# Two weight loads of a cached-attention decode kernel sent in narrow transfers

## The chip, the core and the metric

One core of a Trainium2 chip runs the program. The metric is the device time of one execution in microseconds; the median of three runs before the change is 2498.54 us (2498.37 to 2499.15).

## The reference

Two layers, each an attention block over a cache and a token-mixing block, for a batch of two tokens of width 512, with 32 query heads, 8 cache heads, a cache of 32768 positions and head width 128:

```python
q = (layernorm(x) @ wq)                       # per head of 128
scores = q . k_cache * Dh ** -0.5             # 4 query heads share one cache head
x = x + softmax(scores) @ v_cache @ wo
h = layernorm(layernorm(x))                   # then the mixer, over the token axis
x = x + gelu(h * w1 + b1) @ w2 + b2
```

The caches of keys and values are read in both layers, 268 MB each, in float32; the weights are small beside them.

## The kernel before, in words

All that the loads bring goes into one tile `mem` of 106 cells, each 512 floats wide on all 128 partitions. A unit is one layer, batch and cache head. Its keys (kind K, from `kt`) are 64 cells, its values (kind V, from `v`) as many. A head's `wq` and `wo` parts are 4 cells each (2048 floats, 8 KB on a partition, 1 MB in all), from `wqo`. PE multiplies cell by cell as they come: `k_step` (L360) writes scores, `v_step` (L428) sums up the values, `make_q` makes a unit's queries from `wq` (L325 is its wide product, ten steps of four cells ahead of the unit's first key).

The order of all work is a list of steps written by `Order`: the keys of a unit, then the values of the unit before. `plan_loads` goes through it ahead of time and gives each load a size (32 cells at most, which is 8 MB) and a place among the 106 cells; weights are asked for 16 steps ahead (`ASK_Q`). Some cells are kept over at the two places where a layer ends and the next begins (about 1000 to 1460 us); there the loads are of 4 cells and less. All loads are issued on SP's queue in the planner's order by `load` (L877 weights, L882 caches), each when PE has done with what stood in its cells. The loads take eight completion semaphores in turn (DMAHW0 to DMAHW7 below), and a load waits for the last one that used its semaphore, unless another of its waits covers that. Small inputs and one output row go over ACT's queue.

Each of these loads has 128 partitions, and the sixteen DMA engines take eight rows each; a row is one packet. An engine's part ends in a packet of 4 bytes, which counts up the load's semaphore. PE's instructions come over the same engines (queue q8).

Of the kernel before, what the change touches and what calls it, by code (L numbers as in the profile page):

```python
# [13 lines left out]
P = 128  # L14
G = 512
# [23 lines left out]
STEP_US = 1.6  # L39
ASK_Q = 16  # L40
ASK_O = 8


class Order:
# [158 lines left out]


@with_exitstack
def gqa_mixer_kernel(ctx: ExitStack, tc: tile.TileContext, x, kt, v, wqo, cols, out):
    nc = tc.nc
    B, D = out.shape
    HKV = wqo.shape[0]
# [21 lines left out]
    def cells(a, n):  # L231
        return mem[:, a * G : (a + n) * G]
# [538 lines left out]
    for u in order.units:  # L771
        layer, b, h = u
# [11 lines left out]
    for name, us in users.items():  # L784
        k0 = min(first["K", u] for u in us)
        h = name if isinstance(name, int) else name[1]
# [3 lines left out]
        weights.append((k0 - ASK_Q if k0 else -1, ("q", layer, h), max(first["K", u] for u in us) if both else k0))  # L790
        weights.append((k0 if both else v0 + ASK_O, ("o", layer, h), max(end["V", u, 1] for u in us) + 3))

    for u in order.units:
        layer, b, h = u
# [76 lines left out]
    def load(label, n, a):  # L871
        kind, u, g = label
        if kind == "W":
            part, layer, h = u
            w = D * R
            at_w = 0 if part == "q" else w
            nc.sync.dma_start(cells(a, n), wqo[h][:, at_w : at_w + w])  # L877
            (wq_sb if part == "q" else wo_sb)[layer, h] = cells(a, n).rearrange("p (t c) -> p t c", t=DT)
            return
        layer, b, h = u  # L880
        src = (kt if kind == "K" else v)[b * HKV + h, g // HALF, :, (g % HALF) * G : (g % HALF + n) * G]
        nc.sync.dma_start(cells(a, n), src)  # L882
        for j in range(n):
            at_cell[kind, u, g + j] = a + j
            if (kind, u, g + j) in order.kept:
                at_cell[order.kept[kind, u, g + j]] = a + j
# [5 lines left out]
    for label, n, a in begin.get(-1, ()):  # L892
        load(label, n, a)
# [4 lines left out]
    for p, (kind, u, g) in enumerate(steps):  # L898
        (k_step if kind == "K" else v_step)(u, g)
        for f, args in hooks.pop(p, ()):  # L900
            f(*args)
        for label, n, a in begin.get(p, ()):
            load(label, n, a)
# [3 lines left out]
def _layout(A_x, A_k_cache, A_v_cache, A_wq, A_wo, B_w1, B_b1, B_w2, B_b2):  # L907
    import numpy as np

    B, HKV, SK, DH = A_k_cache.shape  # L910
    D = A_x.shape[-1]
    U = B * HKV
    kt = A_k_cache.reshape(U, 2, NG, 32, 2, 2, 8, 2, 2, DH).transpose(0, 1, 9, 4, 7, 8, 2, 5, 6, 3)
    wq = A_wq.reshape(D // P, P, HKV, -1).transpose(2, 1, 0, 3)
    wo = A_wo.reshape(HKV, -1, DH, D).transpose(0, 2, 1, 3)
    w1, b1, w2 = (a.reshape(P, -1) for a in (B_w1, B_b1, B_w2))
    none = np.zeros_like(w2)
    w2z = np.stack([none, w2], axis=2).reshape(P, -1)
    cols = [w1, b1, w2z, none[:, :1], np.broadcast_to(B_b2.reshape(1, 1), (P, 1))]
    return {  # L920
        "x": np.ascontiguousarray(A_x.reshape(B * (D // P), P).T),
        "kt": np.ascontiguousarray(kt).reshape(U, 2, DH, HALF * G),
        "v": A_v_cache.reshape(U, 2, P, HALF * G),
        "wqo": np.concatenate([wq.reshape(HKV, P, -1), wo.reshape(HKV, DH, -1)], axis=2),
        "cols": np.concatenate(cols, axis=1),
    }


_INS = ["x", "kt", "v", "wqo", "cols"]


# [20 lines left out]
```

## Time and profile before

| what | value |
|---|---|
| profiled execution, device time | 2498.51 us |
| its span, first to last instruction | 2496.7 us |
| moved by DMA | 1064.64 MB, mean 426 GB/s |
| loads on SP's queue (q1) | 34568 packets, 1063.27 MB |
| PE busy | 1335.6 us, 53% |
| mean granted clock of TensorE | 0.765 |
| weight loads | 28, 1024 KB each, median 38.0 us from issue to landing |

The page's DMA line gives the busy share of all sixteen engines in 40 slices of 62.4 us. A query by stretches gives the same share, and GB/s, for any part of the span. Of the time of a single DMA engine there is no view, but the trace holds every packet with its start, duration, size and queue.

### The profile page before, as it was taken

To read this page: it belongs to the slowest core of one execution; us is meant where nothing else is said; L and a number is where in the kernel's file an instruction comes from. 1 tells how busy PE (TensorE), PEld (TensorE's weight loads), DVE (VectorE), ACT (ScalarE), POOL (GpSimd) and SP (SyncE) were. 2 spreads that over 40 slices of the span, in tenths; PEclk is the share of its full clock that TensorE was granted. 3 is DMA by queue.
4 is the path that set the end of the run, shared out by engine and by line. 5 is a ranking of instruction groups with operands and counts; after the bars stand their busy time and mean duration, and the time that the engine had idled before them with its cause. 6 is when DMAs were issued, how large, how long until landed. Compare 5 with 4: busy or idle time off the path is not lost.

```text
span 2496.7 us, 21064 instructions
## 1 busy us (share of the span) xinstructions
PE 1335.6 (53%) x9562; PEld 373.7 (15%) x9562; DVE 211.3 (8%) x599; ACT 186.9 (7%) x581; POOL 5.1 (0%) x18
## 2 busy tenths in 40 slices
PE   3455455444445544556776774454454544554557
PEld 1111111111111111111221221111111111111113
DVE  1000000000000000101110110000000000000012
ACT  0100000000000000000210210000000000000021
POOL 0000000000000000000000000000000000000000
PEclk8777777777777777778887986777677777776788
DMA  9999999999999999999999999999999999999996
GB/s 421 434 433 430 434 431 434 430 431 436 433 427 437 428 434 434 424 436 408 419 429 422 420 427 437 433 433 430 433 434 428 434 432 434 433 433 433 429 433 275
DMA packets 34946, 1064.64 MB, mean 426 GB/s; under 512 B 4133, under 2 KB 4137, under 8 KB 5034
## 3 DMA queue, kind: packets, MB, share of 16 engines
q1 hardware_dynamic: 34568, 1063.27, 99.1%
q8 instruction: 75, 1.23, 0.2%
q14 instruction: 13, 0.11, 0.0%
q10 hardware_dynamic: 290, 0.04, 0.0%
HBM read 1063.29 MB, written 0.00 MB: 426 GB/s over the span
## 4 chain that ended last, share of the span: by engine, by line
DMA 63%; PE 24%; another core or an unknown queue 11%; DVE 1%; issue 0%; ACT 0%; SPq 0%; POOLq 0%; POOL 0%; DVEq 0%; ACTq 0%
DMA mem<-in_v_dram 34%; DMA mem<-in_kt_dram 29%; PE acc L428 15%; PE scores L360 6%; PE misc L332 1%; PE bcast L325 0%; PE rows L492 0%; PE misc L384 0%; PE misc L451 0%; PE misc L657 0%; ACT S L410 0%; PE misc L378 0%; DVE row L462 0%; SPq L882 0%
## 5 line engine op out<-in xcount | busy, mean ns | idle before, releaser
L428 PE MATMUL acc<-mem,S 128*16 128x512 f32 x4080 | 595.5, 716 | 595.4 <-DMA mem<-in_v_dram 587.2
L360 PE MATMUL scores<-mem,qz 128*32 128x512 f32 x4096 | 593.7, 720 | 531.7 <-DMA mem<-in_kt_dram 531.6
L410 ACT ACTIVATE S<-S,neg 128x128 f32<-128x128 f32 x256 | 129.5, 509 | 2212.0 <-DVE S L405 1196.1
L360 PEld LDWEIGHTS scores<-mem,qz 128*32 128x32 f32 x4096 | 141.9, 126 | 910.6 <-issue 820.6
L428 PEld LDWEIGHTS acc<-mem,S 128*16 128x16 f32 x4080 | 127.2, 106 | 907.4 <-issue 827.5
L370 DVE TENSOR_REDUCE mx<-scores 128x1 f32<-128x512 f32 x64 | 44.3, 692 | 795.4 <-PE scores L360 787.6
L405 DVE STREAM_TRANSPOSE S<-scores 128x512 f32<-128x512 f32 x64 | 45.5, 710 | 125.4 <-PE acc L428 125.4
L410 ACT ACTIVATION_READ_ACCUMULATOR S<-S,neg 128x1 f32 x256 | 47.7, 187 | 0.0
L492 PE MATMUL rows<-mem,oz 128*2 128x512 f32 x248 | 46.6, 835 | 0.3 <-DVE oz L481 0.3
L380 DVE TENSOR_REDUCE m<-misc 1x4 f32<-1x128 f32 x32 | 8.9, 279 | 383.3 <-PE misc L378 383.3
L453 DVE RECIPROCAL rl<-misc 128x4 f32<-128x4 f32 x32 | 5.8, 182 | 384.6 <-PE misc L451 384.6
L462 DVE SCALAR_TENSOR_TENSOR row<-acc,quad,row 128x128 f32<-128x128 f32 x96 | 33.7, 351 | 3.4
L460 DVE TENSOR_SCALAR row<-acc,quad 128x128 f32<-128x128 f32 x32 | 11.2, 350 | 174.0 <-PE acc L428 174.0
L481 DVE TENSOR_TENSOR oz<-misc,rl 128x4 f32<-128x4 f32 x32 | 5.2, 161 | 221.3 <-PE misc L471 220.9
L471 PEld LDWEIGHTS misc<-head,row 128*128 128x128 f32 x64 | 14.0, 273 | 52.2 <-issue 38.3
L325 PE MATMUL bcast<-mem,xw 128*32 128x512 f32 x144 | 20.6, 635 | 1.7 <-POOL x_rs L298 1.7
L451 PEld LDWEIGHTS misc<-both,one 128*128 128x128 f32 x64 | 13.6, 266 | 49.9 <-issue 47.0
L471 PE MATMUL misc<-head,row 128*128 128x4 f32 x64 | 16.8, 333 | 7.3 <-DVE row L462 7.3
L332 PEld LDWEIGHTS misc<-selg,row 128*128 128x128 f32 x128 | 17.1, 208 | 20.1 <-issue 11.2
L576 ACT ACTIVATE row<-bcast,bias,scale 128x512 f32<-128x512 f32 x21 | 16.3, 777 | 36.7 <-PE rows L560 13.4
L332 PE MATMUL misc<-selg,row 128*128 128x2 f32 (+1 forms) x128 | 18.5, 266 | 0.8 <-DVE row L317 0.8
L451 PE MATMUL misc<-both,one 128*128 128x4 f32 x64 | 16.4, 327 | 2.0 <-DVE both L450 2.0
(126 smaller groups left out, 277.0 us busy)
## 6 DMA issues: line engine op xcount, KB each, us to landing
mem<-in_v_dram SPq DMA_DIRECT2D x13, 4096.0 KB, 25.5
mem<-in_v_dram SPq DMA_DIRECT2D x37, 1024.0 KB, 9.0
mem<-in_kt_dram SPq DMA_DIRECT2D x15, 2048.0 KB, 17.4
mem<-in_kt_dram SPq DMA_DIRECT2D x30, 1024.0 KB, 8.9
mem<-in_wqo_dram SPq DMA_DIRECT2D x28, 1024.0 KB, 38.0
mem<-in_kt_dram SPq DMA_DIRECT2D x6, 4096.0 KB, 28.7
mem<-in_kt_dram SPq DMA_DIRECT2D x2, 6144.0 KB, 24.1
mem<-in_v_dram SPq DMA_DIRECT2D x3, 2048.0 KB, 38.4
```

Source lines behind the costliest of these rows:

```text
L325: nc.tensor.matmul(q_ps[us][32 * d : 32 * d + 32, :], xw[:, d, :], wq[:, d, :], start=True, stop=True)
L332: nc.tensor.matmul(pt[:, r * n : (r + 1) * n], q_row[us][:, r * DH : (r + 1) * DH], side, start=True, stop=True,)
L360: nc.tensor.matmul(sc_ps[u, half][32 * row : 32 * row + 32, :], qz[:, at : at + 32], cells(at_cell["K", u, g], 1), start=(i == 0), stop=(i ...
L370: nc.vector.tensor_reduce(mx[u][:, half : half + 1], sc_ps[u, half], axis=AX.X, op=ALU.max)
L405: nc.vector.transpose(S[half], sc_ps[u, half])
L410: nc.scalar.activation(s[:, :, h], s[:, :, h], AF.Exp, bias=neg[u][:, h : h + 1], scale=SCALE, accum_out=lsum[u][:, half, h : h + 1],)
L428: nc.tensor.matmul(acc[32 * row : 32 * row + R * QT, :], S[half][:, col : col + R * QT], vc, start=(g < NG), stop=(g >= quads - NG),)
L451: nc.tensor.matmul(pl[:, :R], ones, both, start=True, stop=True)
L462: nc.vector.scalar_tensor_tensor(asb[u], acc[:, t * DH : (t + 1) * DH], quad[:, t : t + 1], asb[u], op0=ALU.mult, op1=ALU.add)
L471: nc.tensor.matmul(po_of[u][:, :R], asb[u], head, start=True, stop=(u != order.last))
L492: nc.tensor.matmul(rows[32 * r : 32 * r + B, :], oT[u][:, 2 * r + 1 - b : 2 * r + 3 - b], wo_of(u)[:, r, :], start=False, stop=(u == order ...
L576: nc.scalar.activation(hid[key, f], px[key], AF.Gelu_apprx_tanh, bias=shift[key][:, f : f + 1], scale=slope[key][:, f : f + 1],)
```

## The change

Two of the 28 weight loads are issued otherwise: `wq` of head 5 in layer 0, and `wq` of head 1 in layer 1. Their partitions 96 to 127 come in one transfer as before (32 rows). Partitions 0 to 95 come in four transfers of 24 partitions, from a new input `narrow`, where the rows lie as six groups of four, with a fifth row of padding behind each group, so that the source's outermost dimension has six members. The change's own words for it are transfers of six DMA engines. Bytes, cells, the plan and the order of all other loads stay as they are.

```diff
+NARROW = (("q", 0, 5), ("q", 1, 1))
+GROUPS = 6
+DEPTH = 4
+PIECES = 4
...
-            nc.sync.dma_start(cells(a, n), wqo[h][:, at_w : at_w + w])
+            if u in NARROW:
+
+                size = GROUPS * DEPTH
+                cut = PIECES * size
+                nc.sync.dma_start(cells(a, n)[cut:, :], wqo[h][cut:, at_w : at_w + w])
+                for k in range(PIECES):
+                    to = cells(a, n)[k * size : (k + 1) * size, :]
+                    nc.sync.dma_start(to, narrow[NARROW.index(u), k][:, :DEPTH, :])
+            else:
+                nc.sync.dma_start(cells(a, n), wqo[h][:, at_w : at_w + w])
...
+    narrow = np.zeros((len(NARROW), PIECES, GROUPS, DEPTH + 1, 4 * G), np.float32)
+    for i, (part, _, h) in enumerate(NARROW):
+        w = (wq if part == "q" else wo)[h].reshape(P, -1)[: PIECES * GROUPS * DEPTH]
+        narrow[i, :, :, :DEPTH] = w.reshape(PIECES, GROUPS, DEPTH, -1)
```

On SP's queue, about 679 to 736 us into the execution, there stood before (behind each row what it waits for: DMAHW a load's completion, PE the freeing of its cells):

```order
L882 DMA mem<-in_kt_dram 128x16384 [waits DMAHW3_49,PE_49]
L877 DMA mem<-in_wqo_dram 128x2048 [waits DMAHW7_49]
L882 DMA mem<-in_v_dram 128x16384 [waits DMAHW4_49,PE_49]
L877 DMA mem<-in_wqo_dram 128x2048 [waits PE_49]
L882 DMA mem<-in_v_dram 128x16384 [waits DMAHW5_49,PE_49]
L882 DMA mem<-in_kt_dram 128x16384 [waits DMAHW6_49,PE_49]
```

and now stands:

```order
L895 DMA mem<-in_kt_dram 128x16384 [waits DMAHW3_49,PE_49]
L885 DMA mem<-in_wqo_dram 32x2048 [waits DMAHW7_49]
L888 DMA mem<-in_narrow_dram 24x1x2048 x4
L895 DMA mem<-in_v_dram 128x16384 [waits DMAHW4_49,PE_49]
L890 DMA mem<-in_wqo_dram 128x2048 [waits DMAHW5_49,PE_49]
L895 DMA mem<-in_v_dram 128x16384 [waits DMAHW6_49,PE_49]
L895 DMA mem<-in_kt_dram 128x16384 [waits DMAHW7_49,PE_49]
```

The four narrow transfers take four semaphores, so the ones behind move up by four. The second V load waited for the load on DMAHW5, the first of the two K loads ahead; it now waits for DMAHW6, the second of them (the first row shown). The wo load between got a wait for the first K load, and the K load at the end waits for the 32-row part instead of the second K load. PE's waits are the same.

The second place, also on SP, about 2030 to 2090 us; before:

```order
L877 DMA mem<-in_wqo_dram 128x2048 [waits DMAHW3_49]
L882 DMA mem<-in_v_dram 128x16384 [waits DMAHW0_49,PE_49]
L877 DMA mem<-in_wqo_dram 128x2048 [waits PE_49]
L882 DMA mem<-in_v_dram 128x16384 [waits DMAHW1_49,PE_49]
L882 DMA mem<-in_kt_dram 128x16384 [waits DMAHW2_49,PE_49]
```

and now:

```order
L885 DMA mem<-in_wqo_dram 32x2048 [waits DMAHW7_49]
L888 DMA mem<-in_narrow_dram 24x1x2048 x4
L895 DMA mem<-in_v_dram 128x16384 [waits DMAHW4_49,PE_49]
L890 DMA mem<-in_wqo_dram 128x2048 [waits DMAHW5_49,PE_49]
L895 DMA mem<-in_v_dram 128x16384 [waits DMAHW6_49,PE_49]
L895 DMA mem<-in_kt_dram 128x16384 [waits DMAHW7_49,PE_49]
```

The same has happened: the second V load waited for the first of the two K loads ahead (DMAHW1 before) and waits for the second of them now (DMAHW6 after). On the other engines only line numbers differ.

More of the change, by code (lines that the diff above doesn't have):

```diff
@@ L205, in gqa_mixer_kernel @@
 @with_exitstack
-def gqa_mixer_kernel(ctx: ExitStack, tc: tile.TileContext, x, kt, v, wqo, cols, out):
+def gqa_mixer_kernel(ctx: ExitStack, tc: tile.TileContext, x, kt, v, wqo, narrow, cols, out):
     nc = tc.nc
@@ L924, in _layout @@
         "wqo": np.concatenate([wq.reshape(HKV, P, -1), wo.reshape(HKV, DH, -1)], axis=2),
+        "narrow": narrow,
         "cols": np.concatenate(cols, axis=1),
     }
-_INS = ["x", "kt", "v", "wqo", "cols"]
+_INS = ["x", "kt", "v", "wqo", "narrow", "cols"]
 def kernel(A_x, A_k_cache, A_v_cache, A_wq, A_wo, B_x, B_w1, B_b1, B_w2, B_b2):
```

## The prediction

> **What bounds the kernel now.** First the page: busy share of the DMA engines in 40 slices, the queues, and the chain that ended last.
>
> ```profile
> DMA  9999999999999999999999999999999999999996
> q1 hardware_dynamic: 34568, 1063.27, 99.1%
> q8 instruction: 75, 1.23, 0.2%
> ...
> DMA 63%; PE 24%; another core or an unknown queue 11%; DVE 1%; issue 0%; ACT 0%; SPq 0%; POOLq 0%; POOL 0%; DVEq 0%; ACTq 0%
> ```
>
> The loads (q1) fill 99.1% of sixteen engines' time and only the last slice isn't full, so nothing but the DMA engines is worth looking at. The q8 row is small but matters below: 75 instruction fetches of 16 KB ride on the same engines. Then the stretches of the span (last two columns: share of sixteen engines, GB/s), the chain in order of time at its end, and the end by the microsecond:
>
> ```profile
> 600.00:1150.00 550.00, 276.98 (x1928) 75.15 (x1928) 38.88 (x109) 28.55 (x109) 0.00 (x0) 0.75 1.00 431
> ```
> ```profile
> 2439.75 39.62 DMA mem<-in_v_dram
> 2479.41 0.45 PE held L437 x8
> ...
> 2493.62 0.35 DVE mem L753
> ```
> ```profile
> 2471.00:2472.00 1.00, 1.00 (x16) 0.26 (x9) 0.00 (x0) 0.00 (x0) 0.00 (x0) 1.00 1.02 412
> 2472.00:2473.00 1.00, 1.00 (x12) 0.21 (x5) 0.00 (x0) 0.00 (x0) 0.00 (x0) 1.00 0.66 268
> 2474.00:2475.00 1.00, 0.62 (x8) 0.25 (x12) 0.00 (x0) 0.00 (x0) 0.00 (x0) 1.00 0.49 205
> 2477.00:2478.00 1.00, 1.00 (x35) 0.71 (x26) 0.80 (x3) 0.00 (x0) 0.00 (x0) 1.00 0.46 176
> 2478.00:2479.00 1.00, 1.00 (x27) 0.68 (x26) 0.00 (x0) 0.00 (x0) 0.00 (x0) 1.00 0.09 35
> ```
>
> One engine moves 431 / 16 = 26.9 GB/s. The last load is issued at 2439.75 and takes 39.62 us to land, all of it time in the engines' own queues; what follows it is 2496.7 − 2479.4 = 17.3 us of fixed chain. And the engines don't finish together: from 2473 to 2478 half of them (share 0.49) are still at it. **Eight engines are late by some six us, and they set the end.** Why, the trace's packet records tell (start us, ns, bytes, queue; each engine's next packet starts as its last ends):
>
> ```
> 48.509 2418 65536 q1     the usual: next packet of this engine at 50.923
> 48.715 1071 16384 q8     a fetch; next packet of this engine at 49.771,
> 49.771 2885 65536 q1     which takes 467 ns too long
> ...
> 2411.523 87 2048 q10     the one output row on ACT's queue
> 2414.028 9 4 q1          that engine's completion of the load then running
> 2413.460 9 4 q1          the same load's first completion, of another engine
> ```
>
> A fetch sets its engine back by 1.06 + 0.47 = 1.5 us. Followed engine by engine, the records put all 75 fetches on the same number of engines, eight, nine or ten each, and none on the other eight. The sixteen completion packets of a load give each engine's lag behind the first:
>
> ```
> load ending at    eight early engines   eight late engines (us)
>  723.8            0.00 to 1.69          3.28 to 4.92
> 1164.3            0.00 to 0.87          4.69 to 5.55
> 2074.5            0.00 to 0.89          3.06 to 4.91
> 2471.9 (last)     0.00 to 1.78          5.36 to 7.03
> ```
>
> Between the second and the third row the lag is lost (a first part already about 1088), since the early ones run dry while SP waits for cells that hang on the late ones:
>
> ```profile
> 1176.00:1177.00 1.00, 1.00 (x10) 0.30 (x2) 0.23 (x1) 0.65 (x3) 0.00 (x0) 1.00 0.93 385
> 1177.00:1178.00 1.00, 0.14 (x5) 0.07 (x8) 0.16 (x1) 1.00 (x5) 0.00 (x0) 0.97 0.73 254
> 1178.00:1179.00 1.00, 1.00 (x8) 0.23 (x12) 0.00 (x0) 0.98 (x3) 0.00 (x0) 0.50 0.82 311
> ```
>
> So the lag is paid twice, once about 1177 and once at the end.
>
> **The change, part by part.** *Moved bytes.* Before, a wq load gives each engine 8 rows of 8 KB. After, 32 rows go to all sixteen (2 each) and 96 rows, in four transfers of 24, to six engines (4 rows each, four times): 18 rows on each of the six, 2 on each of the other ten. At 26.9 GB/s, the six gain 10 rows, 81,920 B or +3.04 us, and the ten lose 6, 49,152 B or −1.82 us, with each load. There is one such load in each half, at 724 and at 2075, so each meets one of the two places where the lag is paid.
>
> If the six are early ones: about 1164 the late eight fall from 4.69–5.55 to 2.87–3.73 and the six rise to at most 0.87 + 3.04 = 3.91. The latest engine goes from 5.55 to 3.91: −1.64 us. At the end the late eight fall to 3.54–5.21, the six rise to at most 1.78 + 3.04 = 4.82: from 7.03 to 5.21, −1.82 us. **Sum −3.46 us.** A bound from the same table: no shift of bytes can bring the latest below the mean lag. With the middles of the four ranges that is about 2.8 at 1164 and 3.5 at the end, so at most 2.8 + 3.5 = 6.3 us.
>
> *A new wait on SP.* Loads take eight completion semaphores in turn, and four more loads take four more of them. The big V load two places behind the wq load therefore waits for a later K load than before (the order's rows in the section on the change). Issues on SP, and PE when that K load has landed:
>
> ```profile
> 678.87 0.41 SPq L877 DMA_DIRECT2D mem<-in_wqo_dram  x1
> 698.10 0.33 SPq L882 DMA_DIRECT2D mem<-in_v_dram  x1
> 713.56 0.33 SPq L877 DMA_DIRECT2D mem<-in_wqo_dram  x1
> 718.90 0.33 SPq L882 DMA_DIRECT2D mem<-in_v_dram  x1
> 735.91 0.33 SPq L882 DMA_DIRECT2D mem<-in_kt_dram  x1
> ```
> ```profile
> 726.85 9.01 PE L360 MATMUL scores<-mem,qz 128*32 128x512 f32 x64 [8.02 <-DMA mem<-in_kt_dram]
> ...
> 758.50 1.04 PE L325 MATMUL bcast<-mem,xw 128*32 128x512 f32 x8
> ```
>
> It was issued at 718.90 and now can't be before about 726.5: 7.6 us later. At the second place:
>
> ```profile
> 2068.36 0.33 SPq L882 DMA_DIRECT2D mem<-in_v_dram  x1
> 2087.14 22.96 SPq L882 DMA_DIRECT2D mem<-in_kt_dram  x2
> ```
> ```profile
> 2077.62 9.45 PE L360 MATMUL scores<-mem,qz 128*32 128x512 f32 x64 [9.33 <-DMA mem<-in_kt_dram]
> ...
> 2107.80 1.04 PE L325 MATMUL bcast<-mem,xw 128*32 128x512 f32 x8
> ```
>
> From 2068.36 to about 2077.3, 8.9 us. I cost both at nothing: at 726.5 every engine still has the 8 MB V load of 698.10 before it, which takes 8.39 MB / 431 GB/s = 19.5 us, so none runs dry before some 740. Queued behind the waiting issue on SP is a K load that went at 735.91 (2087.14) anyway, when PE freed its cells. If the cover were gone, it would cost 7.6 + 8.9 = 16.5 us at most.
>
> *Four more issues on SP* per load, 0.4 us each as the first row has it, 1.6 us: SP stands idle until 698.10 behind them. *Landing of wq itself:* the six engines end it 3 us later, about 730; PE reads it at 758.50 and 2107.80 (L325), 28 us later. *Row size* stays 8 KB, and the bytes read are the same. All nothing.
>
> Forecast by this: 2498.51 (the profiled execution; 2496.7 of span and 1.8 around it; the median of the runs is 2498.54) − 3.46 = **2495.0**.
>
> **The rivals.** *The way into the memory is the bottleneck, not the engine.* The row of 2474 shows eight engines alone at 205 / 8 = 25.6 GB/s, no faster than 26.9: the cap is each engine's, or that of the part of the memory which it alone writes in every load; before never has an engine write another's partitions, so the trace can't tell. The change does that. A transfer of 24 rows is 4 rows per engine, 32,768 B, 1.22 us; if it shares its way with that partition's usual engine, both take 1.22 us longer. For none to all four transfers the six lose 0 to 4.9 us more. I take two of four, the middle: the six gain 3.04 + 2.44 = 5.48. About 1164 the latest is then 0.87 + 5.48 = 6.35 (+0.80), at the end 1.78 + 5.48 = 7.26 (+0.23): 2499.5; with all four 2504.4. For it: 64 KB packets take 2418 to 2431 ns on every engine, as if all met one fixed limit. [...]
> [...]
>
> *Late engines among the six (slower).* Nothing in the trace numbers the engines. One thing is known: the only transfer on a single engine in this kernel (the output row at 2411.523) was carried by an early one, 2414.03 − 2413.46 = 0.57 us behind the first. If a transfer over six takes that engine and five others of which some are late, these pay +3.04 us at both places: with the latest of all +6.1 (2504.6), with the least late one 4.69 + 3.04 − 5.55 = 2.18 and 5.36 + 3.04 − 7.03 = 1.37, so +3.6 (2502.1). It decides as soon as an engine with a lag over 5.55 − 3.04 = 2.5 at 1164 is among the six, and all eight late ones are over that.
> [...]
>
> *It isn't six engines.* If the transfers spread evenly after all, nothing moves and the time stays 2498.5.
>
> **How the numbers follow.** Forecast 0.50 (2495.0, its own range 2493.6 to 2496.8: down to halfway to the floor of 2492.2 that the bound of 6.3 sets, up to half the gain); shared way 0.25 (2499.5, to 2504.4); late engines among the six 0.17 (2502.1 to 2504.6, more if both rivals hold); not six engines 0.08 (2498.5). The range 2493.6 to 2504.6 leaves out the tails, under 2 in 10. The bound of 0.2%, about what a measurement of this kernel tells from no change, is 5.0 us, 2493.5 and 2503.5: faster 0.03 (the forecast's floor), slower 0.13 (the upper part of late engines, 0.09, and of the shared way, 0.04), within it 0.84.
>
> **What would show it.** Right: at the end the stretch of half share (0.49) shrinks from five us to about two, and the dip at 1177 fades. The shared way: rows of the narrow transfers that take twice as long, and a V load whose packets stretch on the other engines about 725. Late engines: the half-share stretch grows to eight or nine us. The new wait wrong: a DMA share under 1 near 745 or 2096. Wrong altogether if the time moves by more than 6.3 us downwards.

## The result, and the profile after

The changed kernel takes **2519.87 us** (median of 5, 2518.16 to 2521.14) against 2498.58 (2498.37 to 2499.22) for the one before on the same chip: a ratio of 1.0082, 95% interval 1.0071 to 1.0094, or +21.3 us. The profiled execution took 2518.16, 19.65 us more than that of before; the sums below are made against these 19.65.

The page of the changed kernel: busy share and GB/s of the engines in 40 slices (62.9 us each), the queues, the chain.

```profile
DMA  9999999999999999999999999999999999999995
GB/s 418 434 434 434 434 432 433 432 429 436 432 395 434 432 433 427 426 431 399 419 431 420 414 432 436 432 433 429 439 433 432 433 432 388 432 433 433 434 428 239
q1 hardware_dynamic: 34616, 1063.27, 98.8%
q8 instruction: 75, 1.23, 0.2%
...
DMA 62%; PE 24%; another core or an unknown queue 12%; DVE 1%; issue 0%; ACT 0%; SPq 0%; POOLq 0%; POOL 0%; DVEq 0%; ACTq 0%
```

By share of time nothing has changed: the engines are as busy as ever, and bytes and fetches are the same. The GB/s tell it: two slices, the 12th and the 34th, fall to 395 and 388, and each holds one narrow load (the 19th, now 399, was at 408 before). Busy, but slower. The same by stretches (share, GB/s), first of before, then of the changed kernel, with three pieces of the first dip:

```profile
700.00:760.00 60.00, 31.25 (x214) 8.50 (x214) 2.38 (x7) 2.11 (x8) 0.00 (x0) 0.72 1.00 430
2070.00:2110.00 40.00, 19.72 (x140) 5.40 (x140) 1.45 (x5) 0.00 (x0) 0.00 (x0) 0.70 1.00 431
```
```profile
700.00:760.00 60.00, 23.05 (x158) 6.00 (x162) 1.70 (x4) 2.11 (x8) 0.00 (x0) 0.69 1.01 395
2070.00:2110.00 40.00, 15.73 (x124) 4.10 (x116) 1.54 (x3) 0.00 (x0) 0.00 (x0) 0.76 1.01 366
...
720.00:724.00 4.00, 0.00 (x0) 0.00 (x0) 0.00 (x0) 0.00 (x0) 0.00 (x0) 0.91 0.95 279
724.00:728.00 4.00, 0.00 (x0) 0.00 (x0) 0.00 (x0) 0.00 (x0) 0.00 (x0) 0.50 1.11 272
728.00:732.00 4.00, 1.74 (x12) 0.51 (x16) 0.00 (x0) 0.00 (x0) 0.00 (x0) 0.50 1.06 248
```

At a share of 1.01, 395 in place of 430 over 60 us is 60 x (1 − 395/430) = 4.9 us lost, and 366 for 431 over 40 us is 6.0. The packet records say where (start and end in us, ns, bytes; the changed kernel):

```
726.069 730.563  4494  65536    a cache load's packet: 2420 before
726.165 730.854  4689  65536
726.248 726.813   565   8192    a narrow load's row: 314 when nothing is in its way
726.302 726.911   609   8192
```

I add up what all 64 KB packets take over 2421 ns and all 8 KB packets over 314 ns, and divide by 16 engines. This **slowed engine time** is 5.64 us at the first load and 6.32 at the second (0.10 and 0.13 before), so **+11.7 us**. The slow packets last as long as rows of the narrow load are under way, from 721.5 to 736.1 and from 2079.9 to 2097.2, and at the height of it all sixteen engines are slow: at 728.0 us six rows of 0.51 to 0.56 us and ten cache packets of 3.7 to 4.8 us are under way.

Then the end, and the place near 1177, which is now near 1185 (share, GB/s):

```profile
2489.00:2490.00 1.00, 1.00 (x12) 0.26 (x8) 0.00 (x0) 0.00 (x0) 0.00 (x0) 1.00 0.62 242
2491.00:2492.00 1.00, 1.00 (x16) 0.26 (x9) 0.00 (x0) 0.00 (x0) 0.00 (x0) 1.00 0.10 43
2492.00:2493.00 1.00, 0.80 (x8) 0.25 (x3) 0.00 (x0) 0.00 (x0) 0.00 (x0) 1.00 0.06 25
2497.00:2498.00 1.00, 1.00 (x27) 0.72 (x26) 0.01 (x1) 0.00 (x0) 0.00 (x0) 1.00 0.06 25
```
```profile
1184.00:1185.00 1.00, 0.30 (x4) 0.16 (x8) 0.96 (x3) 0.00 (x0) 0.00 (x0) 1.00 0.67 279
1185.00:1186.00 1.00, 1.00 (x10) 0.30 (x2) 0.22 (x1) 0.67 (x3) 0.00 (x0) 1.00 0.24 98
1186.00:1187.00 1.00, 0.62 (x9) 0.24 (x12) 0.16 (x1) 1.00 (x5) 0.00 (x0) 1.00 0.57 106
```

The stretch of eight engines at share 0.49 is gone. In its place **one engine alone** (0.06 is 1/16) works on for 6.5 us, from 2491.5 to 2498.0, at 25 GB/s. From 2440 to the last packet an engine is idle for 25.2 us on average, before 19.7: **+5.5**. Near 1185 nearly all engines run dry, and from 1160 to 1200 the idle time is 1.54 us per engine against 0.37: **+1.2**. Together 11.7 + 5.5 + 1.2 = 18.4 of the 19.65; the rest lies in pieces of half a us and less.

The completions at 1164 say the same: fifteen engines within 2.2 us (1164.12 to 1166.29), and one 6.9 us behind the first. Seven of the eight late ones have been relieved, one has not.

The new wait, on SP's queue and on PE:

```profile
678.91 3.23 SPq L888 DMA_DIRECT2D mem<-in_narrow_dram  x4
697.85 0.37 SPq L895 DMA_DIRECT2D mem<-in_v_dram  x1
713.54 0.33 SPq L890 DMA_DIRECT2D mem<-in_wqo_dram  x1
730.19 0.33 SPq L895 DMA_DIRECT2D mem<-in_v_dram  x1
...
2088.37 0.33 SPq L895 DMA_DIRECT2D mem<-in_v_dram  x1
```
```profile
730.26 8.65 PE L364 MATMUL scores<-mem,qz 128*32 128x512 f32 x64 [11.64 <-DMA mem<-in_kt_dram]
```
```profile
736.00:744.00 8.00, 2.91 (x28) 0.67 (x20) 0.85 (x2) 0.00 (x0) 0.00 (x0) 0.98 0.96 412
744.00:752.00 8.00, 0.00 (x0) 0.00 (x0) 0.00 (x0) 0.00 (x0) 0.00 (x0) 0.50 0.91 393
752.00:760.00 8.00, 3.56 (x20) 0.88 (x24) 0.00 (x0) 0.00 (x0) 0.00 (x0) 0.50 1.12 483
```

The V load goes out when the K load has landed, at 730.19, as forecast but later, since that landing is late itself. No stretch behind it is empty: the three shares, 0.96, 0.91 and 1.12, are 1.00 on average.

### The profile page after: what moved, and what is told of

The parts are those of the page before. It is cut to its first block, busy times and chain, and to the rows that moved or that the text cites. A ratio compares the mean times of both kernels' runs of the same rounds, so it can differ in the third digit from the quotient of the medians.

```text
span 2516.4 us, 21079 instructions
## 1 busy us (share of the span) xinstructions
PE 1333.5 (53%) x9562; PEld 374.8 (15%) x9562; DVE 211.4 (8%) x599; ACT 186.9 (7%) x581; POOL 5.2 (0%) x18
## 3 DMA queue, kind: packets, MB, share of 16 engines
q1 hardware_dynamic: 34616, 1063.27, 98.8%
## 4 chain that ended last, share of the span: by engine, by line
DMA 62%; PE 24%; another core or an unknown queue 12%; DVE 1%; issue 0%; ACT 0%; SPq 0%; POOLq 0%; POOL 0%; DVEq 0%; ACTq 0%
DMA mem<-in_kt_dram 34%; DMA mem<-in_v_dram 29%; PE acc L432 12%; PE scores L364 9%; PE rows L496 0%; PE misc L336 0%; PE bcast L329 0%; PE misc L388 0%; PE misc L475 0%; PE misc L661 0%; PE misc L455 0%; DVE row L466 0%; PE rows L727 0%; ACT S L414 0%
## 5 line engine op out<-in xcount | busy, mean ns | idle before, releaser
L464 DVE TENSOR_SCALAR row<-acc,quad 128x128 f32<-128x128 f32 x32 | 11.2, 351 | 173.2 <-PE acc L432 173.2
```

## The experiments

Two questions: what slows the packets (other engines' partitions, uneven shares, the source in groups, the new waits), and whose is the tail? Times are medians; slowed engine time is for both loads together (0.2 in the kernel before). e1, e2, e5 to e9 and e12 leave out part of the two loads, 77 to 104 of the 128 rows of each. That alone makes them shorter: the 80 rows that e1, e2 and e5 leave out of each load are 1.31 MB, 3.0 us at 431 GB/s.

| run | us | ratio to before, 95% | slowed engine time, us |
|---|---|---|---|
| e1_own | 2497.87 | 0.9995 [0.9986, 1.0004] | 0.2 |
| e2_foreign | 2508.68 | 1.0037 [1.0024, 1.0051] | 7.7 |
| e3_split16 | 2511.15 | 1.0046 [1.0031, 1.0061] | 12.3 |
| e4_columns | 2499.70 | 1.0002 [0.9992, 1.0012] | 0.3 |
| e5_near | 2507.68 | 1.0037 [1.0022, 1.0051] | 4.1 |
| e6_one_far | 2517.05 | 1.0071 [1.0056, 1.0086] | 6.0 |
| e7_one_near | 2514.54 | 1.0060 [1.0045, 1.0075] | 4.7 |
| e8_half_dose | 2501.33 | 1.0009 [0.9999, 1.0018] | 4.5 |
| e9_five_own | 2493.57 | 0.9980 [0.9970, 0.9989] | 0.2 |
| e10_first | 2509.24 | 1.0041 [1.0026, 1.0056] | 6.0 |
| e11_second | 2508.85 | 1.0040 [1.0025, 1.0055] | 6.2 |
| e12_three_far | 2505.19 | 1.0027 [1.0016, 1.0038] | 12.1 |
| e13_five | 2508.63 | 1.0038 [1.0023, 1.0052] | 12.3 |

The kernel before took 2498.81 beside e1 to e4, 2499.26 beside e5 to e8, 2498.77 beside e9 to e12 and 2498.68 beside e13.

### Own partitions or others': e1_own, e2_foreign

The narrow part alone, 48 rows of each load, once to partitions 0 to 23 and 32 to 55, once to 64 to 87 and 96 to 119. Source in groups, engines, bytes and semaphores are the same in both; STARTS is (0, 32), then (64, 96).

```diff
-                nc.sync.dma_start(cells(a, n)[cut:, :], wqo[h][cut:, at_w : at_w + w])
-                for k in range(PIECES):
-                    to = cells(a, n)[k * size : (k + 1) * size, :]
+                for k, at in enumerate(STARTS):
+                    to = cells(a, n)[at : at + GROUPS * DEPTH, :]
                     nc.sync.dma_start(to, narrow[NARROW.index(u), k][:, :DEPTH, :])
```

Expected of e1_own:

> Two of the narrow transfers of each of the two loads are kept, moved to partitions 0 to 23 and 32 to 55; the other 80 rows of the two loads are left out (1.3 MB less in all). [...] By the theory that the six engines, or the padded source, are what is slow: half of the 21 us of loss stays, 2505 to 2510, with 64 KB packets of 3.5 us and more near 720 and 2080. By the theory of the new wait: no loss, since fewer loads stand in the queue.

Expected of e2_foreign:

> The same two transfers, the same source, six engines and bytes as e1_own, but on partitions 64 to 87 and 96 to 119, which other engines write in every whole load; 80 rows left out as there. Shared way: 64 KB packets stretch to 3.5 us and more, 2505 to 2512. Six engines or the source are slow: the same time as e1_own. New wait: the same as e1_own.

One stretch of each (share, GB/s), e1_own first:

```profile
724.00:728.00 4.00, 1.17 (x8) 0.45 (x12) 0.00 (x0) 0.00 (x0) 0.00 (x0) 0.50 1.06 459
```
```profile
724.00:728.00 4.00, 0.00 (x0) 0.00 (x0) 0.00 (x0) 0.00 (x0) 0.00 (x0) 0.50 1.02 276
```

10.8 us lie between the two, and only the partitions differ. With 0 to 23 and 32 to 55 no packet is slow, and by this alone they are called the six engines' own, four in a row to an engine; with 64 and up 64 KB packets take 3.7 to 4.9 us, and of those that start from 722 to 726 none takes 2.42. 7.5 of the 10.8 us are slowed engine time. Of the rest, 2.1 us are in the tail, where one engine is alone for some three us, and 1.0 is between the median of e1_own and its profiled execution (2498.91). The shared way is the reading that fits, and what is slowed reaches further than thought: by fours a transfer's 24 partitions would be those of six others, which would leave four engines that share nothing (an estimate from e1_own; no run shows whose the partitions from 64 up are), and yet no packet is spared: at 724 us five rows and eleven cache packets of 3.7 to 4.9 us are under way, sixteen in all. The source in groups is cleared by e1_own. In e1_own the completions also show who the six are: five early ones, and one 3.1 us behind the first.

### Even shares, and columns: e3_split16, e4_columns

The whole load both times: as 32 and 96 rows, from the old source, over all sixteen engines; and as five transfers of all 128 partitions, cut by columns.

```diff
-                for k in range(PIECES):
-                    to = cells(a, n)[k * size : (k + 1) * size, :]
-                    nc.sync.dma_start(to, narrow[NARROW.index(u), k][:, :DEPTH, :])
+                nc.sync.dma_start(cells(a, n)[:cut, :], wqo[h][:cut, at_w : at_w + w])
```
```diff
-                nc.sync.dma_start(cells(a, n)[cut:, :], wqo[h][cut:, at_w : at_w + w])
-                for k in range(PIECES):
...
+                for c, k in ((0, 512), (512, 512), (1024, 512), (1536, 256), (1792, 256)):
+                    nc.sync.dma_start(cells(a, n)[:, c : c + k], wqo[h][:, at_w + c : at_w + c + k])
```

Expected of e3_split16:

> The two loads whole, from the old source, each as one transfer of 96 rows and one of 32, so that sixteen engines have even shares (6 and 2 rows) but mostly on partitions that they don't write in a whole load. Shared way: stretched packets and a loss like the change's, 2508 to 2520. Six engines (uneven shares) or the padded source: no loss, 2498 to 2500. New wait: one more load in the queue, no loss, 2498 to 2500.

Expected of e4_columns:

> The two loads whole, from the old source, each as five transfers of all 128 partitions and 512, 512, 512, 256 and 256 columns: as many loads and semaphores in SP's queue as the change has, but even shares on their usual partitions. New wait on SP: a good part of the loss is here, 2505 to 2520. Shared way, six engines, source: no loss, 2498 to 2500 (rows of 2 KB and 1 KB cost a little more, under 1 us).

The stretches of e3_split16:

```profile
700.00:760.00 60.00, 24.83 (x164) 6.65 (x168) 2.21 (x6) 2.11 (x8) 0.00 (x0) 0.66 1.01 393
2070.00:2110.00 40.00, 13.56 (x104) 3.53 (x96) 1.54 (x3) 0.00 (x0) 0.00 (x0) 0.69 1.00 363
```

By the split of the transfers, 6 and 2 rows to an engine, every engine carries 8 rows, as before, but six in a row are not the four in a row of e1_own, so most of them should be for partitions that it doesn't write in a whole load. The dips are those of the changed kernel, the slowed engine time 12.3 − 0.2 = 12.1, and the time +12.3: here the whole loss is slowed engine time, with no narrow transfer at all. And e4_columns has the five issues and the later V load without foreign partitions:

```profile
678.32 2.31 SPq L883 DMA_DIRECT2D mem<-in_wqo_dram  x5
...
727.20 0.33 SPq L890 DMA_DIRECT2D mem<-in_v_dram  x1
```

The V load is 8.3 us later than before (10.1 at the second place) and the kernel takes +0.9 us, within an interval of −2.0 to +3.0. So the new wait and the issues are cleared of all but a small part of the 21.3 us. The smaller rows cost little: in the kernel before a packet of 2 KB on q1 takes 84 ns (24.4 GB/s), one of 8 KB 312 ns (26.3).

### How far it reaches: e5_near, e6_one_far, e7_one_near, e8_half_dose, e12_three_far

e5_near and e8_half_dose are e1_own with STARTS (4, 36) and (64,). The other three send one transfer of rows from the old source, 64 to 94, 0 to 30 and 64 to 114 (ONE is (64, 95), (0, 31), (64, 115)):

```diff
+                lo, hi = ONE
+                nc.sync.dma_start(cells(a, n)[lo:hi, :], wqo[h][lo:hi, at_w : at_w + w])
```

Expected of e5_near:

> Leaves out 80 of the 128 rows of the two loads: only 48 rows come, in two narrow transfers each, to partitions 4 to 27 and 36 to 59. That is the transfers of the earlier experiment on partitions 0 to 23 and 32 to 55, which cost nothing, moved by four partitions: each of the six engines writes four partitions that its neighbour in number writes in every whole load, all in the lower half of the memory. Theory A (a foreign row holds up all sixteen engines, whosever it is): the 64 KB packets of about 720 to 731 take 3 to 5 us on all engines as with partitions 64 to 119, and the time is 2507 to 2510. Theory B (only the two engines on one way hold each other up): five or six ways are shared, four rows at a time, at most 1.2 us per transfer; some 64 KB packets stretch and at least nine engines' packets stay at 2.42 us; 2498 to 2501. Theory C (it is the crossing from one half of the partitions to the other that clogs): no packet stretches beyond 2.5 us or so, and 2497.9 as before.

Expected of e6_one_far:

> Leaves out 97 of the 128 rows of the two loads: one transfer of 31 rows to partitions 64 to 94. 31 is a prime, so by the way the transfers of 24 went to six engines this one goes to a single engine (9.6 us of its time if nothing is in its way; if it is spread over more, the completions show it). Theory A (a foreign row holds up all sixteen engines): while it lasts, the 64 KB packets of all engines take clearly more than 2.42 us, and the GB/s fall well under 400 for 10 to 20 us. Theory B (only the two engines on one way): at any time one other engine's packet is long, the GB/s stay over 380 and the others at 2.42 us. Time: the one engine sends 31 rows instead of 8, +7.2 us, and is one of the early ones, so about 2498.5 to 2502 by B; 2503 to 2510 by A.

Expected of e7_one_near:

> The same with partitions 0 to 30, so that the single engine writes four rows of its own and 27 of its neighbours in the same half of the memory (97 rows are left out). Theory A: as with partitions 64 to 94. Theory B: as there, too. Theory C (crossing between the halves): no packet stretches here, and the time is the one of the far transfer by B, 2498.5 to 2502.

Expected of e8_half_dose:

> Leaves out 104 of the 128 rows of the two loads: one narrow transfer each, 24 rows to partitions 64 to 87, half of what cost 9.9 us (both loads) with partitions 64 to 87 and 96 to 119. If the price goes by the number of foreign rows: +5 us, 2503 to 2504, and a slow stretch half as long (some 5 us instead of 10). If it is a price per load, whatever is in it: still about 2507 to 2509. If it takes several transfers in a row to clog the way: under 2500.

Expected of e12_three_far:

> Leaves out 77 of the 128 rows of the two loads: one transfer of 51 rows (3 times 17) to partitions 64 to 114, by the earlier transfers on three engines with 17 rows each. One engine with foreign rows made the 64 KB packets of the uninvolved engines 2.72 us instead of 2.42, and of the one whose partitions it wrote 3.8 us. If the slowing of the uninvolved grows with the number of engines that write foreign rows: about 3.0 to 3.4 us for most packets while it lasts (some 10 us). If it is there or not there: 2.7 us again. Time, with about 10 rows more on three engines at twice their time: 2507 to 2513.

A step of four partitions is enough: in e5_near all eleven cache packets under way at 724 us take 2.9 to 3.3 us (up to 3.7 at the second load, single ones 4.5 to 4.8), less than the 3 to 5 of theory A, but on every engine. Each against its own kernel before, it takes 9.4 us more than e1_own. Of these 3.9 are slowed engine time, and idle engines add 2.6 from 770 to 1200 and 2.6 at the end. All of these partitions are under 64, so it isn't the crossing into the other half (theory C falls, here and in e7_one_near, with 4.7 us of slowed time). The clearest view is e6_one_far, where a single engine sends 31 rows (start and end in us, ns, bytes; the records have no partitions, so whose are written is read from the 3.9 us that a packet takes while four rows are under way):

```
723.851 727.757  3906  65536    the engine whose partitions are being written
724.338 725.032   694   8192    a foreign row
725.017 725.719   702   8192
725.135 727.897  2762  65536    an engine that has no part in it
725.704 726.358   654   8192
726.353 726.766   413   8192    four rows, then the next engine's partitions
726.692 730.591  3899  65536    the next engine that is written over
```

Two things are in it. *The way itself:* in 3.9 us 64 KB and four rows, 32 KB, went by this reading into one engine's partitions, 98,304 B / 3.9 us = 25.2 GB/s from two engines, hardly less than the 26.9 of an engine by itself. That much is theory B. *The rest:* the uninvolved engines need 2.65 to 2.77 us, 9 to 14% more than 2.42, and that is theory A. The 31 rows took 18.1 us in place of 31 x 0.314 = 9.7. e6_one_far and e7_one_near came out at 2517.05 and 2514.54, well over what I had expected (2510 at most), because one engine that is 18 us late is paid for at both places: from 770 to 1200 and at the end the engines are idle for some 5.6 and 8.1 us longer than before.

With three engines (e12_three_far) packets take 4.7 to 4.9 us, as with six far ones (e2_foreign), though only three write foreign rows: more than the 3.4 us I had allowed. The time, 2505.19, is under the 2507 to 2513 that I expected: of the 12.1 us of slowed time, 2.9 come back as bytes left out (77 rows per load), and about 2.3 less than before is lost from 1000 to 1500 and at the end. If the three take the rows in order, the first and the third write partitions 34 apart. Those might by turns be one engine's, if from 64 up partitions 32 apart have one engine as 0 to 3 and 32 to 35 have in e1_own; that is a guess which no run shows. Single rows take up to 0.99 us there. Half the rows (e8_half_dose) gave 4.5 us of slowed time for 7.7, and 2501.33, less than the 2503 to 2504 expected from half the price. Of the difference 0.9 us are bytes, 24 rows per load fewer than in e2_foreign; the rest is not explained. The slowed time goes roughly by the rows.

By what path the uninvolved engines of e6_one_far are slowed (2.65 to 2.77 us for 2.42), no run here shows, and how the slowing grows with the number of writers (2.7 us with one, 2.9 to 3.5 with six neighbours, 4.8 with three or six far ones) stays open.

### Whose tail: e9_five_own, e10_first, e11_second, e13_five

e9_five_own is e1_own with five groups, 20 rows per transfer. e10_first and e11_second keep one of the two narrow loads, the first by the diff, the second with the other entry alone:

```diff
-NARROW = (("q", 0, 5), ("q", 1, 1))
+NARROW = (("q", 0, 5),)
```

Expected of e9_five_own:

> Leaves out 88 of the 128 rows of the two loads: two narrow transfers of 20 rows, five groups of four, to partitions 0 to 19 and 32 to 51, where the transfers of 24 rows to partitions 0 to 23 and 32 to 55 showed five early engines and one late one (its completion 3.1 us behind the first) and no slow packet. If the late engine was the sixth in number: five completions within about 1.3 us, none late, and the late eight are all relieved of eight rows (2.4 us) at both places, so up to 2 us less than that experiment's 2497.9: 2495.5 to 2497.5. If it is one of the first five: one of the five completions is again about 3 us behind, and the time is 2497 to 2498.5.

Expected of e10_first:

> The changed kernel with only the load of layer 0 in narrow transfers; the one of layer 1 is whole again. Theory A (the packets of all engines are slowed while foreign rows are on their way, 5.6 us here, and one late engine among the six is paid where the lag is paid): 5.6 us, 1 to 2 us of dry engines near 1186, and at the end the old stretch of eight late engines: 2506 to 2508. Theory B (only uneven shares cost, at the places where the lag is paid): half of the whole, 2509, and no slow stretch about 725. Theory C (relief of the late engines works, as predicted, and the rest is from the second load): under 2499.

Expected of e11_second:

> The changed kernel with only the load of layer 1 in narrow transfers. Theory A: 6.3 us of slowed packets, and at the end one engine alone for some 8 us, 5 to 6 us more of idle engines there than before: 2509.5 to 2511.5, and with the first one alone the two sums make up the 21 us of both. If the tail of one engine needs both loads: 2504 to 2506.

e9_five_own against e1_own is the neatest pair. The engines' completions of the narrow rows at the first load (us):

```
723.88 724.47 724.76 724.89 725.12 726.97    e1_own, six engines
723.84 724.42 724.76 724.90 725.04           e9_five_own, five engines
```

Without the sixth engine none is late, so the late engine among the six is **the sixth**. Its eight rows per load, 131 KB in all, are 0.3 us when spread evenly, and the time goes from 2497.87 to 2493.57 (2 us below what I had expected of the run). Eight rows are 8 x 8192 B / 26.9 GB/s = 2.4 us of one engine; paid twice that is 4.9, and measured are 4.3. The places don't split it evenly, though: between the two profiled executions, 5.5 us apart, the engines' idle time at the end differs by 0.9 us only. The rest lies from 1000 to 1500: 1.4 us of idle time, and 3.1 us of slowed 8 KB packets of the small loads there (up to 2.1 us each near 1220 and 1380 in e1_own). That the lag is paid at both places fits; that each pays 2.4 us is not shown. It also fits that e1_own gains only 0.9 us over the kernel before for the 3.0 us of bytes that it leaves out, and e9_five_own 5.2 for 3.3: in e1_own the sixth engine keeps its eight rows.

One load alone gives 2509.24 or 2508.85. The excesses, 10.5 and 10.1 us, make up nearly the 21.3 of both, though only the slowed packets add up place by place. The first has the old tail of eight late engines at the end, and the second the new one (share, GB/s; e10_first, then e11_second):

```profile
2486.00:2487.00 1.00, 1.00 (x14) 0.32 (x7) 0.00 (x0) 0.00 (x0) 0.00 (x0) 1.00 0.47 193
2488.00:2489.00 1.00, 1.00 (x27) 0.72 (x20) 0.57 (x2) 0.00 (x0) 0.00 (x0) 1.00 0.47 182
```
```profile
2483.00:2484.00 1.00, 1.00 (x12) 0.34 (x4) 0.00 (x0) 0.00 (x0) 0.00 (x0) 1.00 0.23 92
2486.00:2487.00 1.00, 1.00 (x13) 0.42 (x6) 0.19 (x1) 0.00 (x0) 0.00 (x0) 1.00 0.06 25
2489.00:2490.00 1.00, 0.77 (x30) 0.26 (x20) 0.00 (x0) 0.00 (x0) 0.00 (x0) 1.00 0.07 23
```

e10_first is 1 to 3 us above what I expected; its engines run dry by small amounts at several places from 1000 to 1500, 2.7 us in all more than before, and another 2.6 us are slowed packets there. Together that is 5.3 us where the changed kernel loses 2.2. e11_second is 0.7 us below the 2509.5 that I expected at least.

Last, the changed kernel without the sixth engine, the whole load (the part over all sixteen engines grows from 32 to 48 rows):

```diff
-GROUPS = 6
+GROUPS = 5
```

Expected of e13_five:

> The changed kernel with five engines in place of six: four transfers of 20 rows (five groups of four) and 48 rows over sixteen engines (three each), the whole load. The sixth in number is the late engine, as the transfers of 20 and of 24 rows to the engines' own partitions showed. Theory A (slowed packets are one cost, the late engine among the six another): the slow stretches stay, some 11 to 12 us of engine time for both loads, but no single engine works on alone for 8 us at the end: 2509 to 2513.5. Theory B (the cost beyond the slowed packets comes from the uneven shares, whoever carries them): the tail stays, 2517 to 2521.

2508.63, 11.2 us under the changed kernel, with as much slowed engine time (12.3). The end of it (share, GB/s):

```profile
2488.00:2489.00 1.00, 1.00 (x12) 0.37 (x7) 0.00 (x0) 0.00 (x0) 0.00 (x0) 0.75 0.66 258
2489.00:2490.00 1.00, 1.00 (x9) 0.24 (x2) 0.00 (x0) 0.00 (x0) 0.00 (x0) 0.75 0.38 143
2490.00:2491.00 1.00, 1.00 (x12) 0.56 (x14) 0.00 (x0) 0.00 (x0) 0.00 (x0) 0.75 0.04 14
```

No engine works on alone, though five of them still carry 19 rows per load and the others 3. (This profiled execution had a granted clock of 0.648, 0.76 in the others, and took 2516.26 us, the other four 2507.67 to 2509.04; so only the transfers are read from it.) The tail was the sixth engine's, not that of uneven shares. That +9.95 is less than the 12.1 of slowed time points to a relief of the late engines by some 2 us, but the interval of the ratio is wider than that.

## Why the prediction was wrong, point by point

- *Nothing but the DMA engines bounds it:* right. The chain and the shares are the old ones.
- *The lag of the late engines is paid twice:* borne out in sum by e9_five_own against e1_own (4.3 us for one engine's 2.4). In the traces the end pays 0.9 of it and the stretch from 1000 to 1500 most of the rest, so that the sum comes out near twice 2.4 is in part luck.
- *A transfer of 24 rows takes six engines with four rows each:* right. The changed kernel has 48 more packets on q1, which are the 4-byte completions of six engines for each of eight transfers (34616 for 34568), and the counts of e13_five, e12_three_far and e6_one_far fit five, three and one engine.
- ***"If the six are early ones"* failed.** Five are, the sixth is not. The prediction had this as a rival at 2502.1 to 2504.6, so 7.1 to 9.6 us over its forecast; taking the sixth engine out gave 11.2. That it is more is probably because its 18 rows took 0.56 to 0.59 us each on average in place of 0.314; no run separates the two. The reason given for "early", that the one row on ACT's queue ran on an early engine, held for that one engine alone, and said nothing of the sixth.
- ***"The cap is each engine's"* failed, and it is the larger error.** In e6_one_far 25.2 GB/s went from two engines into what reads as one engine's partitions, no more than one alone moves (26.9). The rival had this mechanism, but mis-sized: 1.22 us per shared transfer, as lag on the six, 4.9 us at most in a load. It took two of the four transfers as shared, the middle, which no run shows; by e1_own the six engines' own partitions are 0 to 23 and 32 to 55, and as the groups of four fall (a step of four is enough, e5_near) only the first transfer goes to its engines' own, so three are shared, which by the rival's sum gives 2502.0 in place of 2499.5. Measured are 5.64 and 6.32 us *on the mean of all sixteen engines*, which no relief of single ones can get back. Two more things were missing in the sum. The 32-row part, two rows per engine where the own ones are four in a row, should write foreign partitions as well (no run has it alone); only the four transfers of 24 were counted. And packets of engines that share no way were taken to go on at 2.42 us; all sixteen were slow, with cache packets of up to 4.9 us at the first load and 5.3 at the second.
- *What would show it:* the mark that the prediction set for the shared way, rows twice as long and V packets that stretch about 725, is what came: 0.56 and 0.59 us a row.
- *The new wait, the four issues, the landing of wq cost nothing:* right as far as e4_columns tells for the first two. The issues took 3.23 us for four, 0.8 each and not 0.4. The last row of wq landed at 736.1, later than the 730 forecast, but in the changed kernel PE reads it at 765.22, 29 us later.
- *Chances:* each rival was given under 0.3 and they were weighed against each other. They are no alternatives: one concerns the way into the memory, the other who carries the rows. Both hold, they add up and probably multiply (a late engine's rows are slowed as well), and the time lies 15 us above the range: "more if both rivals hold" stood there without a number.

## What to carry to other kernels

Where the DMA engines set the time, as here (q1 99.1%), let each engine write the partitions that it writes in every other load: cut a load by columns (e4_columns, +0.9 us), not by partitions (e3_split16, +12.3 us for two loads of 1 MB). Keep two accounts in such a sum: bytes per second of all engines together, and the lag of single ones; a change that mends the second can spoil the first (here seven of eight late engines relieved, and +11.7 us of slowed engine time). And before bytes are moved between engines, find out with a small transfer to their own partitions which of them are late: its completions tell (e1_own, one 3.1 us behind the first).

## What the runs showed of the hardware

- In the changed kernel, whose narrow rows go mostly to partitions of other engines, all sixteen were slow meanwhile: 248 to 279 GB/s at the first load (720 to 732 us) and 217 to 293 at the second (2080 to 2092), in place of 430, at a busy share of 0.95 to 1.14. With one such engine (e6_one_far) the packets of uninvolved ones took 2.65 to 2.77 us for 2.42.
- Into what reads as the partitions of one engine went 25.2 GB/s from two engines (e6_one_far), against 26.9 of one alone. By that, rows moved from a late engine to an early one stayed on the same way: in the changed kernel a narrow row took 0.56 and 0.59 us for 0.314.
- Of the eight engines that the instruction fetches (q8) hold up, by 1.5 us with each fetch, one is the sixth of the six on which the narrow transfers ran: followed from packet to packet in the changed kernel, the engine whose row ends last at the first load (736.08) carries the fetches of 271.3, 555.9, 859.9 and 1146.4, every eighth of all. The first five, by their early completions in e1_own and e9_five_own, are not among them.
- No kernel with the whole load was found that beats the one before. e9_five_own (2493.57) leaves out 88 rows per load.
